# Weight tiles kept in HBM as float32r parts, and an ordering model with other matmul durations and one resource shared by DVE's SBUF and POOL's operations

## The chip, the cores and the metric

The kernel runs on one core of a Trainium2 chip. The metric is the time of one execution on the device in microseconds, the median of several runs.

## The reference

Four sequences of 576 positions pass through three layers in a row.

- Attention: 8 heads of 64 features; scores `q k^T / 8`, a causal mask, and a bias `min(-(cum_i - cum_j), 0)` from the running sum of `max(s, 0)`; a softmax; the product with `v`.
- A layer norm over 512 features with a gain, `max(xn @ w1a, 0) @ w2a` with 2048 hidden features, added to x (below: layer 0).
- A mixer along the sequence, `u = x + (x^T U V)^T` with rank 32, then `max(u @ w1b, 0) @ w2b`, added to u (below: layer 1).

The weights and U and V arrive as float64, the rest as float32. The result is float32.

```python
x = np.ascontiguousarray(attn_out.transpose(0, 2, 1, 3)).reshape(B, S, H * D)
x = _moe_ref(x=x, **moe_kwargs)       # layer norm, then x + relu(xn @ w1) @ w2
return _moe2_ref(x=x, **moe2_kwargs)  # u = x + (x^T U V)^T, then u + relu(u @ w1) @ w2
```

## The kernel before

The work is cut into eight blocks: each sequence has a part A of 256 positions and a part B of 320. A step is one block with one of the 16 weight tiles of a layer (128 hidden features): `mlp1` makes the hidden features, `mlp2`, two steps behind it (`LAG`), adds them into the output. `GROUPS` lists the order: layer 0 of A0, A1, A2, B0 and A3, layer 1 of A0 and B0 together, layer 0 of B1 and B2, layer 1 of A1 and B1, layer 0 of B3, and layer 1 of the rest, 256 steps in all. Each run takes first the half of the weights that is on chip from the run before, and so loads eight tiles per 16 steps (or per 32, where two blocks run together).

Products are made in float32r, a shorter float that TensorE takes at full pace. To keep the accuracy, a number is split in a high part and a low part (the rest), and a product takes three matmuls: high by high, low by high, high by low (lines 1013 to 1015 in `mlp1`, 1047 to 1049 in `mlp2`). A step has 24 of them. The first two steps take plain float32 (`FULL_STEPS`).

A weight tile has two halves (of w1 and of w2), each 128 x 512. Eight tiles (`WSLOTS`, 16 buffers `w` of a high and a low part) are on chip. A half comes on chip in one of two ways:

- *Fresh*: the raw float64 is loaded (`w_raw`, 512 KB, lines 479 and 481, buffers `wr`), turned to float32 by five operations (`f64_to_f32`, lines 459 to 469: one on ACT or DVE, two on DVE (462, 466), one on ACT (464), and an integer addition on POOL (469)) in a buffer `wt`, and split: the high part is a rounding copy on ACT (343) or DVE (344), the low part a subtraction on POOL (350) or DVE (348). If the tile is used again, the float32 in `wt` is also stored to an HBM buffer `w_dr` (256 KB, line 521).
- *Reloaded*: the float32 is loaded from `w_dr` into a `wt` (256 KB, line 502) and split again.

The first eight tiles of layer 1 (`early`) are converted ahead of time, beside layer 0 (`w_convert`, from step 44 on; layer 1 begins at step 80), and stored (line 491), and their first use is a reload.

Beside the steps runs the rest: attention of the next blocks (scores into PSUM, bias, mask on POOL, maximum on DVE in line 658, exponential on ACT, transposes, the product with v), the layer norms and the mixer. `AT` and `LN` say beside which steps.

Nothing of this is issued in program order. `Plan` records each operation with the engines that may take it and a duration on each (`alts`), and what it reads and writes. `Plan.plan` then runs a model: at each turn the earliest operation that can start is issued, by priority among the ready ones. Where several engines may take one, the one that ends first is chosen, with a price per engine and 10 us window added. `issue` plans once, and then up to six times (`PASSES`) more with the latest starts of the last plan as priorities and with prices moved so that DVE, ACT and POOL are used evenly in each window; the shortest plan is issued. Each engine then works its operations off in that order and waits on semaphores. All DMAs are issued by one queue, SP's, in the order of the plan; in the model a DMA takes 1.1 us and its bytes at 360 per ns. A load has a `gate`: it is not issued ahead of a certain step.

The model knows a matmul as

```python
def mm_cost(n):
    return max(106.7, n / 2.4) + 2.5
```

and treats DVE and POOL as independent of each other. A buffer becomes free when all recorded users of the old tile in it are done; the next tile's first operation waits for that. For `wt` the user is the split, for `w` the last matmul that reads the tile.

Of the kernel before, what the change touches and what calls it, by code (L numbers as in the profile page):

```python
# [9 lines left out]
F32 = mybir.dt.float32  # L10
# [32 lines left out]
def mm_cost(n):  # L43
    return max(106.7, n / 2.4) + 2.5
# [15 lines left out]
WIN, NW = 10e3, 110  # L60


class Buf:
    """A tile that is allocated when the first operation on it is issued."""
# [14 lines left out]
class Op:  # L79
    __slots__ = ("prio", "alts", "deps", "after", "wait", "ready", "bufs", "start", "end", "soft", "eng", "slots", "nbytes", "seq", "gate")  # L80


class Plan:
    """Records operations in program order, then issues them in the order in which a model of
    the engines finds them ready, by priority where several are."""
# [53 lines left out]
    def plan(self, prio, price):  # L139
        """The order in which a model of the engines finds the operations ready, by priority where several are."""  # L140
# [36 lines left out]
        while avail:  # L177
# [3 lines left out]
            for o in avail:  # L181
                fin = None
                for e, (dur, _) in o.alts.items():
                    s = slot(o, e)
                    if s is None:
                        continue
                    s = max(s, o.ready[e])
                    f0 = max(s, tent.get(e, 0.0)) + dur
                    if len(o.alts) > 1:
                        f0 += price[e][min(int(s / WIN), NW - 1)] * dur + (o.soft if e == "dve" else 0.0)  # L190
                    if fin is None or f0 < fin[0]:
                        fin = (f0, max(s, free[e]), e, dur)
# [3 lines left out]
                if fin[1] <= tent.get(e, 0.0):  # L196
                    tent[e] = tent.get(e, 0.0) + fin[3]
# [40 lines left out]
    def latest(self, order, end):  # L238
        """Latest starts that keep the end and the tensor engine's order."""
# [16 lines left out]
    def issue(self, warm):  # L256
        """Plans several times, with the latest starts of the last plan as priorities and engines' prices
        that even their use out, and issues the shortest plan."""
        self.link()
        price = {e: [0.0] * NW for e in ("act", "pool", "pe", "sp")}  # L260
        price["dve"] = [1.0] * NW
        shared = ("dve", "act", "pool")
# [3 lines left out]
        for _ in range(PASSES):  # L266
            prio = self.latest(order, end)
            use = {e: [0.0] * NW for e in price}
            for o, e, *_ in order:
                use[e][min(int(o.start / WIN), NW - 1)] += o.alts[e][0] / WIN  # L270
# [12 lines left out]
        for o, e, s, t, new in best:  # L283
            # Before the first MLP, the tensor engine's gaps are filled, so that its clock stays up.
# [14 lines left out]
def mha_ffn_mixer_ffn(ctx: ExitStack, tc, qkv_p, qkv_a, qkv_b, s, g, w1, w2, U, V, out):  # L299
# [26 lines left out]
    def dve(prio, n, fn, reads, writes, rate=1.042, fixed=68):  # L326
        P.op(prio, {"dve": (fixed + rate * n, fn)}, reads, writes)
# [13 lines left out]
    def copy(prio, n, out, a, reads, writes, psum=False, soft=0.0, slow=False):  # L341
# [3 lines left out]
        }, reads, writes, soft=soft)  # L345

    def tt(prio, n, out, a, b, op, reads, writes, psum=False, soft=0.0):
# [3 lines left out]
        P.op(prio, alts, reads, writes, soft=soft)  # L351
# [85 lines left out]
    for n, it in enumerate(inst):  # L437
        k = (it["l"], it["m"])
        it["fresh"], it["keep"] = k not in seen, False
        if k in seen:  # L440
            inst[seen[k]]["keep"] = True
            if k not in w_dr:
                w_dr[k] = P.fixed(dr_p.tile([128, 1024], F32, name=f"w_dr{k[0]}_{k[1]}"))
# [4 lines left out]
    early = [(1, m) for m in range(HALF)]  # L448
    for it in inst:
        if (it["l"], it["m"]) in early:  # L450
            it["fresh"] = False

    def f64_to_f32(prio, n, dst, raw, bd, br, words=(0, 1)):
        """Bits of float64 in word pairs, rounded to float32."""
# [6 lines left out]
        }, [(br, words[1])], [bd])  # L461
# [24 lines left out]
    def w_convert(prio, l, m, half, gate):  # L486
        raw = w_raw(prio, l, m, half, gate)
        src = P.buf("wt", [128, 512])
        f64_to_f32(prio, 512, lambda: src.tile, lambda: raw.tile, src, raw)
        sl = slice(512 * half, 512 * (half + 1))  # L490
        load(prio, 128 * 2048, lambda: nc.sync.dma_start(w_dr[l, m][:, sl], src.tile), [src], [(w_dr[l, m], half)])

    def w_load(n, half, gate):
# [3 lines left out]
        sl = slice(512 * half, 512 * (half + 1))  # L497
        if it["fresh"]:
            raw = w_raw(prio, l, m, half, gate)
        else:  # L500
            raw = P.buf("wt", [128, 512])
            load(prio, 128 * 2048, lambda: nc.sync.dma_start(raw.tile, w_dr[l, m][:, sl]), [(w_dr[l, m], half)], [raw], gate)
        it["raw", half] = raw

    def w_split(n, half):
        it = inst[n]
        l, m = it["l"], it["m"]
        prio = it["first"] - 4
        src = it.pop(("raw", half))
        sl = slice(512 * half, 512 * (half + 1))  # L510
        if it["fresh"]:
            if it["full"]:
                w = it["w", half] = it["w", 0] if half else P.buf("w", [128, 2, 512])
# [677 lines left out]
```

## Time and profile before

| | before |
|---|---|
| median of 3 runs | 1199.7 us (1198.89 to 1199.91) |
| profiled execution, first to last instruction | 1201.9 us |
| TensorE (PE) busy | 1119.7 us, 7801 matmuls |
| VectorE (DVE) busy | 874.7 us |
| ScalarE (ACT) busy | 652.4 us |
| GpSimd (POOL) busy | 605.7 us |
| DMA | 177.44 MB, mean 148 GB/s |
| mean granted TensorE clock | 0.974 |

The page gives no other time of the profiled execution than its span, so the span stands for it; it is 2.2 us over the median. Busy time of an engine counts from an instruction's start to its end, waits for a resource inside an instruction included. A matmul's end is modelled, and matmuls overlap. The words in front of and behind `<-` are the buffer written and the buffers read: `w<-wt,w` is a split, `wt<-wr` a conversion, `wt<-w_dr` a reload.

### The profile page before, as it was taken

Reading aid. Unit: us, or ns where it says so; the run is one execution under the profiler, and the core shown is the slowest. Engines: PE = TensorE matmul, PEld = TensorE weight load, DVE = VectorE, ACT = ScalarE, POOL = GpSimd, SP = SyncE. Lnnn points to the kernel's source line nnn. Section 1 sums busy time; section 2 is a strip of 40 time slices with the busy share of each in tenths; the row PEclk is TensorE's granted clock in tenths of the full one; section 3 lists DMA queues with packets and bytes.
Section 4 is the critical chain, followed back from the end, with each engine's and each line's share of the span. In section 5 each row is a group of like instructions: output and inputs, shape, how many; then the busy total and the mean of one; then the engine's idle time right before and its main releaser. Section 6 shows DMA issues by size and latency. Waiting matters only on the chain.

```text
span 1201.9 us, 22316 instructions
## 1 busy us (share of the span) xinstructions
PE 1119.7 (93%) x7801; PEld 1049.2 (87%) x7801; DVE 874.7 (73%) x1947; ACT 652.4 (54%) x1484; POOL 605.7 (50%) x717
## 2 busy tenths in 40 slices
PE   8798787998889998998899999999999999999998
PEld 5567687887888988897789898989999999999998
DVE  6999999998997998979997857696664443313232
ACT  5657576786666766756577646474533342312221
POOL 4666666775566665736755644354441362201300
PEclk8879899999999999999899999999999999999999
DMA  6466657334475746526634431734214453311111
GB/s 215 161 229 215 215 193 224 100 132 160 139 241 167 249 166 220 177 78 220 218 102 167 150 109 65 247 120 159 71 54 140 163 173 100 114 45 63 64 43 40
DMA packets 80639, 177.44 MB, mean 148 GB/s; under 512 B 10064, under 2 KB 17744, under 8 KB 80528
## 3 DMA queue, kind: packets, MB, share of 16 engines
q1 hardware_dynamic: 80528, 176.03, 43.7%
q8 instruction: 61, 1.00, 0.3%
q14 instruction: 50, 0.41, 0.1%
HBM read 147.61 MB, written 28.39 MB: 146 GB/s over the span
## 4 chain that ended last, share of the span: by engine, by line
PE 53%; DVE 30%; issue 6%; ACT 5%; DMA 4%; POOL 2%; SPq 0%; POOLq 0%; DVEq 0%; ACTq 0%
PE ps L1013 8%; PE ps L1014 7%; PE ps L1015 7%; PE acc L1047 5%; PE acc L1049 5%; PE acc L1048 5%; DVE t L658 4%; PE ps L1047 2%; PE ps L1048 2%; PE ps L1049 2%; DVE wt L466 2%; PE ps L750 2%; DVE t L612 2%; DVE w L348 2%; DVE hl L1020 2%
## 5 line engine op out<-in xcount | busy, mean ns | idle before, releaser
L350 POOL TENSOR_TENSOR w<-wt,w 128x512 fp32r<-128x512 f32 x173 | 234.8, 1363 | 205.7 <-ACT w L343 122.0
L1013 PE MATMUL ps<-xh,w 128*128 128x256 f32 (+1 forms) x1016 | 314.8, 310 | 2.6 <-DVE mx L658 1.2
L1015 PE MATMUL ps<-xl,w 128*128 128x256 f32 (+1 forms) x1016 | 303.4, 299 | 1.2 <-DVE xl L348 0.9
L1014 PE MATMUL ps<-xh,w 128*128 128x256 f32 (+1 forms) x1016 | 303.1, 298 | 0.0
L1020 DVE SCALAR_TENSOR_TENSOR hl<-ps,hh 128x256 fp32r<-128x256 f32 (+1 forms) x254 | 115.5, 455 | 206.8 <-ACT hh L1019 204.9
L1019 ACT ACTIVATE hh<-ps 128x256 fp32r<-128x256 f32 (+1 forms) x254 | 103.2, 406 | 281.8 <-PE ps L1015 280.3
L1047 PE MATMUL acc<-hh,w 128*128 128x256 f32 (+1 forms) x760 | 230.0, 303 | 6.8 <-DVE x L1057 4.2
L1049 PE MATMUL acc<-hl,w 128*128 128x256 f32 (+1 forms) x760 | 224.6, 296 | 9.1 <-DVE hl L1020 9.0
L1048 PE MATMUL acc<-hh,w 128*128 128x256 f32 (+1 forms) x760 | 223.4, 294 | 0.0
L1013 PEld LDWEIGHTS ps<-xh,w 128*128 128x128 f32 x1016 | 195.0, 192 | 9.4 <-issue 2.4
L1015 PEld LDWEIGHTS ps<-xl,w 128*128 128x128 f32 x1016 | 195.0, 192 | 2.0 <-DVE xl L348 1.3
L1014 PEld LDWEIGHTS ps<-xh,w 128*128 128x128 f32 x1016 | 195.1, 192 | 0.9 <-issue 0.2
L1049 PEld LDWEIGHTS acc<-hl,w 128*128 128x128 f32 x760 | 146.4, 193 | 11.2 <-DVE hl L1020 11.2
L1047 PEld LDWEIGHTS acc<-hh,w 128*128 128x128 f32 x760 | 146.3, 193 | 9.8 <-ACT hh L1019 6.8
L343 ACT ACTIVATE w<-wt 128x512 fp32r<-128x512 f32 x208 | 125.9, 625 | 41.6 <-POOL wt L469 24.7
L1048 PEld LDWEIGHTS acc<-hh,w 128*128 128x128 f32 x760 | 146.5, 193 | 0.5
L670 ACT ACTIVATE t<-t,mx 64x576 f32<-64x576 f32 (+3 forms) x160 | 95.9, 600 | 64.1 <-POOL mx L666 35.2
L469 POOL TENSOR_TENSOR wt<-wt,wr 128x512 int32<-128x512 int32 (+2 forms) x71 | 98.7, 1391 | 50.0 <-DVE wt L466 14.4
L348 DVE TENSOR_TENSOR w<-wt,w 128x512 fp32r<-128x512 f32 x111 | 99.8, 908 | 5.7 <-ACT w L343 4.0
L653 PE MATMUL ps<-kv,q 128*128 128x288 f32 (+4 forms) x320 | 71.2, 337 | 13.4 <-DVE q L348 4.2
L1047 PE MATMUL ps<-hh,w 128*128 128x320 f32 x256 | 79.3, 310 | 0.0
L1049 PE MATMUL ps<-hl,w 128*128 128x320 f32 x256 | 79.3, 310 | 0.0
(149 smaller groups left out, 2133.8 us busy)
## 6 DMA issues: line engine op xcount, KB each, us to landing
wt<-w_dr SPq DMA_DIRECT2D x232, 256.0 KB, 3.0
raw<-qkv_b SPq DMA_DIRECT2D x32, 608.0 KB, 4.6
w_dr<-wt SPq DMA_DIRECT2D x64, 256.0 KB, 2.6
wr<-w1a SPq DMA_DIRECT2D x20, 512.0 KB, 4.2
wr<-w2a SPq DMA_DIRECT2D x20, 512.0 KB, 4.1
nckb<-nck_dr SPq DMA_DIRECT2D x32, 288.0 KB, 5.3
wr<-w1b SPq DMA_DIRECT2D x16, 512.0 KB, 4.8
wr<-w2b SPq DMA_DIRECT2D x16, 512.0 KB, 5.0
```

Source lines behind the costliest of these rows:

```text
L343: "act": ((51 if psum else 94) + 0.8333 * n, lambda: nc.scalar.activation(out(), a(), AF.Copy)),
L348: alts = {"dve": (68 + 1.042 * n, lambda: nc.vector.tensor_tensor(out=out(), in0=a(), in1=b(), op=op))}
L350: alts["pool"] = (148 + 2.104 * n, lambda: nc.gpsimd.tensor_tensor(out=out(), in0=a(), in1=b(), op=op))
L469: P.op(prio, {"pool": (148 + 2.104 * n, lambda: nc.gpsimd.tensor_tensor(out=dst().bitcast(I32), in0=dst().bitcast(I32), in1=pair(0).bitcas ...
L1013: nc.tensor.matmul(ps[:, :n], w[:, 0, sl], xh[:, k, :n], start=k == 0, stop=False)
L1014: nc.tensor.matmul(ps[:, :n], w[:, 1, sl], xh[:, k, :n], start=False, stop=False)
L1015: nc.tensor.matmul(ps[:, :n], w[:, 0, sl], xl[:, k, :n], start=False, stop=k == KT - 1)
L1019: act(st - 1000, n, lambda: nc.scalar.activation(hh[:, :n], ps[:, :n], AF.Relu), [ps], [hh], 51)
L1020: dve(st - 1000, n, lambda: nc.vector.scalar_tensor_tensor(out=hl[:, :n], in0=ps[:, :n], scalar=0.0, in1=f(hh[:, :n]), op0=ALU.max, op1=AL ...
L1047: nc.tensor.matmul(a, w[:, 0, sl], hh[:, :n], start=new, stop=False)
L1048: nc.tensor.matmul(a, w[:, 1, sl], hh[:, :n], start=False, stop=False)
L1049: nc.tensor.matmul(a, w[:, 0, sl], hl[:, :n], start=False, stop=last and (z == 1 or blk == "B"))
```

## The change

- `w_load` of a tile that is not fresh now allocates the buffer `w` and loads both parts into it in one DMA of 512 KB; nothing is computed. `w_dr` has room for the two parts of the two halves.
- `w_split` of a fresh tile converts and splits as before and then stores both parts from `w` (512 KB) if the tile is used again. The store of the plain float32 is gone, also for the tiles of the first two steps.
- `w_convert`, `early` and the steps that ran it are gone: the first use of each tile of layer 1 is fresh.
- `mm_cost` adds 13.3 instead of 2.5.
- An operation has a set `port`: the engines on which it holds a shared resource called "port". POOL holds it in every operation, DVE in those that read no PSUM buffer (marked by the helpers, or by hand where an operation is recorded directly). In the model, two operations that hold it never run at the same time. The prices even out DVE, ACT and the port instead of DVE, ACT and POOL; DVE's price starts at 0.5 instead of 1; and there are 130 windows instead of 110.
- Comments and texts of documentation were taken out.

The model decides the order in which instructions are issued on each engine, and on which engine some of them run. The core of the diff:

```diff
 def mm_cost(n):
-    return max(106.7, n / 2.4) + 2.5
+    return max(106.7, n / 2.4) + 13.3
...
-WIN, NW = 10e3, 110
+WIN, NW = 10e3, 130
...
-    def op(self, prio, alts, reads=(), writes=(), nbytes=0, gate=None, soft=0.0, hold=()):
+    def op(self, prio, alts, reads=(), writes=(), nbytes=0, gate=None, soft=0.0, hold=(), port=False):
         o = Op()
+        o.port = {e for e in alts if e == "pool" or (e == "dve" and port)}
...
-                    f0 = max(s, tent.get(e, 0.0)) + dur
+                    port = e in o.port
+                    f0 = max(s, tent.get(e, 0.0), tent.get("port", 0.0) if port else 0.0) + dur
                     if len(o.alts) > 1:
-                        f0 += price[e][min(int(s / WIN), NW - 1)] * dur + (o.soft if e == "dve" else 0.0)
+                        w = min(int(s / WIN), NW - 1)
+                        f0 += (price[e][w] + (price["port"][w] if port else 0.0)) * dur + (o.soft if e == "dve" else 0.0)
                     if fin is None or f0 < fin[0]:
-                        fin = (f0, max(s, free[e]), e, dur)
+                        fin = (f0, max(s, free[e], free["port"] if port else 0.0), e, dur)
...
             free[e] = o.end
+            if e in o.port:
+                free["port"] = o.end
...
-        price = {e: [0.0] * NW for e in ("act", "pool", "pe", "sp")}
-        price["dve"] = [1.0] * NW
-        shared = ("dve", "act", "pool")
+        price = {e: [0.0] * NW for e in ("act", "pool", "pe", "sp", "port")}
+        price["dve"] = [0.5] * NW
+        shared = ("dve", "act", "port")
...
     def dve(prio, n, fn, reads, writes, rate=1.042, fixed=68):
-        P.op(prio, {"dve": (fixed + rate * n, fn)}, reads, writes)
+        on_chip = not any((b[0] if isinstance(b, tuple) else b).tag in ("ps", "acc") for b in reads)
+        P.op(prio, {"dve": (fixed + rate * n, fn)}, reads, writes, port=on_chip)
...
-    early = [(1, m) for m in range(HALF)]
-    for it in inst:
-        if (it["l"], it["m"]) in early:
-            it["fresh"] = False
...
     def w_load(n, half, gate):
         it = inst[n]
         l, m = it["l"], it["m"]
-        prio = it["first"] - 4
-        sl = slice(512 * half, 512 * (half + 1))
         if it["fresh"]:
-            raw = w_raw(prio, l, m, half, gate)
-        else:
-            raw = P.buf("wt", [128, 512])
-            load(prio, 128 * 2048, lambda: nc.sync.dma_start(raw.tile, w_dr[l, m][:, sl]), [(w_dr[l, m], half)], [raw], gate)
-        it["raw", half] = raw
+            it["raw", half] = w_raw(it["first"] - 4, l, m, half, gate)
 
-    def w_split(n, half):
+    def w_split(n, half, gate):
...
+        dr = w_dr.get((l, m))
+        if not it["fresh"]:
+            w = it["w", half] = P.buf("w", [128, 2, 512], F32R)
+            load(prio, 128 * 4096, lambda: nc.sync.dma_start(f(w.tile), dr[:, half]), [(dr, half)], [w], gate)
+            return
+        raw = it.pop(("raw", half))
+        if it["full"]:
+            w = it["w", half] = it["w", 0] if half else P.buf("w", [128, 2, 512])
+            f64_to_f32(prio, 512, lambda: w[:, half], lambda: raw.tile, (w, half), raw)
+            return
+        w = it["w", half] = P.buf("w", [128, 2, 512], F32R)
+        t = P.buf("wt", [128, 512])
+        f64_to_f32(prio, 512, lambda: t.tile, lambda: raw.tile, t, raw)
+        split(prio, 512, lambda: w[:, 0], lambda: w[:, 1], lambda: t.tile, [t], [(w, 0)], [(w, 1)])
+        if it["keep"]:
+            load(prio, 128 * 4096, lambda: nc.sync.dma_start(dr[:, half], f(w.tile)), [w], [(dr, half)])
...
-    for n, (l, m) in enumerate(early):
-        for half in range(2):
-            put(start1 - 36 + 3 * (n + half / 2), lambda p, g, l=l, m=m, half=half: w_convert(p, l, m, half, g))
```

## Rows read from the trace of the kernel before

**Rows 1.** The page: busy shares, and the chain that ended last.

```profile
PE 1119.7 (93%) x7801; PEld 1049.2 (87%) x7801; DVE 874.7 (73%) x1947; ACT 652.4 (54%) x1484; POOL 605.7 (50%) x717
...
PE 53%; DVE 30%; issue 6%; ACT 5%; DMA 4%; POOL 2%; SPq 0%; POOLq 0%; DVEq 0%; ACTq 0%
```

**Rows 2.** Stretch, length, busy us (count) PE PEld DVE ACT POOL, PEclk, DMA, GB/s.

```profile
0.00:180.00 180.00, 150.37 (x917) 121.31 (x918) 164.92 (x379) 114.47 (x300) 115.53 (x129) 0.89 0.62 205
180.00:420.00 240.00, 215.83 (x1534) 199.86 (x1533) 216.98 (x525) 166.57 (x396) 160.24 (x201) 0.99 0.53 176
420.00:600.00 180.00, 162.62 (x1153) 152.82 (x1152) 162.85 (x328) 112.97 (x238) 112.58 (x132) 0.96 0.54 181
600.00:900.00 300.00, 292.37 (x2028) 277.74 (x2027) 224.73 (x521) 177.81 (x377) 147.22 (x200) 1.00 0.37 125
900.00:1200.00 300.00, 298.46 (x2179) 297.49 (x2177) 105.23 (x200) 80.63 (x175) 70.13 (x57) 1.00 0.28 94
540.00:600.00 60.00, 49.17 (x326) 46.73 (x325) 58.30 (x99) 35.50 (x73) 41.30 (x37) 0.91 0.65 219
840.00:900.00 60.00, 60.00 (x446) 58.79 (x445) 38.29 (x91) 29.14 (x64) 24.69 (x28) 1.00 0.19 65
```

**Rows 3.** Timeline, 555 to 563: start, length, engine, line, operation [idle before].

```profile
555.42 0.68 DVE L466 SCALAR_TENSOR_TENSOR wt<-wr,wt 128x512 uint32<-128x512 uint32 x1
...
556.23 1.38 POOL L469 TENSOR_TENSOR wt<-wt,wr 128x512 int32<-128x512 int32 x1 [2.20 <-ACT xc L843]
...
556.76 1.40 DVE L466 SCALAR_TENSOR_TENSOR wt<-wr,wt 128x512 uint32<-128x512 uint32 x1
...
558.12 0.28 PE L1013 MATMUL ps<-xh,w 128*128 128x256 f32 x1
...
558.24 0.28 PE L1014 MATMUL ps<-xh,w 128*128 128x256 f32 x1
...
558.84 0.31 PE L1047 MATMUL acc<-hh,w 128*128 128x320 f32 x1
...
558.99 0.31 PE L1048 MATMUL acc<-hh,w 128*128 128x320 f32 x1
```

**Rows 4.** Groups by form: line, engine, names, shapes, count | busy, mean ns | idle.

```profile
L350 POOL TENSOR_TENSOR w<-wt,w 128x512 fp32r<-128x512 f32 x173 | 234.8, 1363 | 205.7 <-ACT w L343 122.0 <-DVE w L344 45.5 <-DVE hl L1020 25.1
...
L343 ACT ACTIVATE w<-wt 128x512 fp32r<-128x512 f32 x208 | 125.9, 625 | 41.6 <-POOL wt L469 24.7 <-DMA wt<-w_dr 15.7 <-PE ps L1049 0.4
...
L348 DVE TENSOR_TENSOR w<-wt,w 128x512 fp32r<-128x512 f32 x111 | 99.8, 908 | 5.7 <-ACT w L343 4.0
...
L469 POOL TENSOR_TENSOR wt<-wt,wr 128x512 int32<-128x512 int32 x68 | 96.5, 1420 | 47.8 <-DVE wt L466 13.5 <-ACT wr L464 4.8 <-issue 4.8
...
L466 DVE SCALAR_TENSOR_TENSOR wt<-wr,wt 128x512 uint32<-128x512 uint32 x68 | 60.6, 893 | 0.6
...
L344 DVE CAST w<-wt 128x512 fp32r<-128x512 f32 x76 | 44.5, 589 | 8.6 <-PE ps L1015 4.6 <-DMA wt<-w_dr 2.5 <-POOL wt L469 1.2
...
L462 DVE TENSOR_SCALAR wt<-wt 128x512 uint32<-128x512 uint32 x68 | 44.3, 654 | 5.0 <-ACT wt L459 4.8
```

**Rows 5.** Line 502 in 180 to 420, then 600 to 900: issues, times.

```profile
L502 SPq DMA_DIRECT2D wt<-w_dr x44: 319/320/433, 190.9 to 419.7; - x44
...
L502 SPq DMA_DIRECT2D wt<-w_dr x80: 319/320/889, 605.2 to 882.1; - x80
```

**Rows 6.** Waits of the SP queue: total us, times, longest.

```profile
SPq L502 <- POOL w L350: 225.3, 88, 21.0
SPq L1061 <- DVE x L1057: 136.4, 17, 24.5
```

**Rows 7.** DMA issues: count, KB each, median us to landing.

```profile
wt<-w_dr SPq DMA_DIRECT2D x232, 256.0 KB, 3.0
...
w_dr<-wt SPq DMA_DIRECT2D x64, 256.0 KB, 2.6
...
wr<-w2b SPq DMA_DIRECT2D x16, 512.0 KB, 5.0
```

More of the change, by code (lines that the diff above doesn't have):

```diff
@@ L79 @@
 class Op:
-    __slots__ = ("prio", "alts", "deps", "after", "wait", "ready", "bufs", "start", "end", "soft", "eng", "slots", "nbytes", "seq", "gate")
+    __slots__ = ("port", "prio", "alts", "deps", "after", "wait", "ready", "bufs", "start", "end", "soft", "eng", "slots", "nbytes", "seq", "gate")
 class Plan:
@@ L195, in plan @@
                 e = fin[2]
-                if fin[1] <= tent.get(e, 0.0):
-                    tent[e] = tent.get(e, 0.0) + fin[3]
+                for g in (e, "port") if e in o.port else (e,):
+                    if fin[1] <= tent.get(g, 0.0):
+                        tent[g] = tent.get(g, 0.0) + fin[3]
                 if e not in best:
@@ L269, in issue @@
             for o, e, *_ in order:
-                use[e][min(int(o.start / WIN), NW - 1)] += o.alts[e][0] / WIN
+                w = min(int(o.start / WIN), NW - 1)
+                use[e][w] += o.alts[e][0] / WIN
+                if e in o.port:
+                    use["port"][w] += o.alts[e][0] / WIN
             for w in range(NW):
@@ L344, in copy @@
             "dve": (68 + (1.042 if psum or slow else 0.521) * n, lambda: nc.vector.tensor_copy(out(), a())),
-        }, reads, writes, soft=soft)
+        }, reads, writes, soft=soft, port=not psum)
     def tt(prio, n, out, a, b, op, reads, writes, psum=False, soft=0.0):
@@ L350, in tt @@
             alts["pool"] = (148 + 2.104 * n, lambda: nc.gpsimd.tensor_tensor(out=out(), in0=a(), in1=b(), op=op))
-        P.op(prio, alts, reads, writes, soft=soft)
+        P.op(prio, alts, reads, writes, soft=soft, port=not psum)
     def split(prio, n, hi, lo, src, reads, wh, wl, psum=False, soft=0.0, slow=False):
@@ L442, in mha_ffn_mixer_ffn @@
             if k not in w_dr:
-                w_dr[k] = P.fixed(dr_p.tile([128, 1024], F32, name=f"w_dr{k[0]}_{k[1]}"))
+                w_dr[k] = P.fixed(dr_p.tile([128, 2, 2, 512], F32, name=f"w_dr{k[0]}_{k[1]}"))
         elif n >= 4:
@@ L508, in w_split @@
         prio = it["first"] - 4
[L509 to L513, printed above, removed]
-                f64_to_f32(prio, 512, lambda: w[:, half], lambda: src.tile, (w, half), src)
-                if it["keep"]:
-                    load(prio, 128 * 2048, lambda: nc.sync.dma_start(w_dr[l, m][:, sl], w[:, half]), [(w, half)], [(w_dr[l, m], half)])
-                return
-            raw, src = src, P.buf("wt", [128, 512])
-            f64_to_f32(prio, 512, lambda: src.tile, lambda: raw.tile, src, raw)
-            if it["keep"]:
-                load(prio, 128 * 2048, lambda: nc.sync.dma_start(w_dr[l, m][:, sl], src.tile), [src], [(w_dr[l, m], half)])
-        w = P.buf("w", [128, 2, 512], F32R)
-        split(prio, 512, lambda: w[:, 0], lambda: w[:, 1], lambda: src.tile, [src], [(w, 0)], [(w, 1)])
-        it["w", half] = w
+        dr = w_dr.get((l, m))
[14 more added lines that the diff above has]
+            load(prio, 128 * 4096, lambda: nc.sync.dma_start(dr[:, half], f(w.tile)), [w], [(dr, half)])
     xt = {}
@@ L845, in layer_norm @@
                                                                             scalar2=None, op0=ALU.mult)),
-            }, [(xc, k), g_sb], [(xc, k)])
+            }, [(xc, k), g_sb], [(xc, k)], port=True)
         y, z = P.buf("ls", [128, 320]), P.buf("ls", [128, 320])
@@ L1087, in w_step @@
     def w_step(k, gate):
-        w_split(*halves[k])
+        w_split(*halves[k], gate)
         w_next(k + 2, gate)
```

16 lines of the change are left out of this document (5 added, 11 removed).

## The prediction

> **What bounds the kernel now.** I read the busy shares and the chain of waits first. TensorE (PE) is busy 93% of the span, and the chain that ended last lies 53% on PE and 30% on VectorE (DVE) [rows 1]. So PE sets the end, but DVE makes it late for a good part of the time. Next I read the table by stretch, to see where. From 900 us on PE is busy 298.5 of 300 us and nothing else matters; before 600 us DVE is at 90% or more of each stretch [rows 2].
>
> Busy time flatters PE, because a matmul's record covers its latency. The timeline shows the real pace: starts 0.12 us apart for 256 columns and 0.15 for 320 [rows 3] (0.120 and 0.147 in the unrounded starts). I took the usual interval of each form, over all 7801 matmul starts, and summed what lies above it. That is PE's loss: 63 us in 0 to 180, 47 in 180 to 420, 35 in 420 to 600, 25 in 600 to 900, and 1 after 900, 171 in all. The matmul counts agree: 446 matmuls fit into 840 to 900, where PE is busy throughout, 0.134 us each, and the 1534 of 180 to 420 would need 206 of their 240 us [rows 2]. Spells at the lower granted clock (0.89 on average before 180, 0.91 in 540 to 600) are inside the loss.
>
> The loss follows DVE's load [rows 2]. Per 60 us it is 2.3 us where DVE is at 64% (840 to 900), 5.0 at 75% (600 to 900), 11.7 at 90% (180 to 600), and 18 at 97% (540 to 600). I use these four points as the price list.
>
> Part of DVE's load is waiting. At 556.76 an L466 starts while POOL is in an L469 that ends at 557.61; it ends at 558.16 and takes 1.40 us, where the same instruction took 0.68 just before [rows 3]. So DVE, working on SBUF alone, stood until POOL was done. Over the trace L466 averages 0.893 and the split's subtraction on DVE 0.908 [rows 4], against 0.68 and 0.69 when free. Over L344, L348, L462 and L466 the excess makes about 68 us.
>
> **What is removed.** 232 half tiles are reloaded as float32 and split again (a rounding to the high part, a subtraction for the low part). 16 of them become first uses that are converted and split on the spot, and 216 come back as finished parts. There are 284 splits now: the high part 208 times on ACT at 0.625 and 76 times on DVE at 0.589, the low part 173 times on POOL at 1.363 and 111 times on DVE at 0.908 [rows 4]. 216 of 284 is 76%, so ACT loses 99 us, DVE 111 and POOL 179. Per reload that is 0.51 us of DVE and 0.83 of POOL. What it is worth depends on the stretch.
>
> **180 to 420 us (loss 47).** 44 reloads lie here [rows 5]: 22 us of DVE go. The early conversion of layer 1's first eight tiles also goes from here, 16 halves with 0.654 + 0.893 of DVE each [rows 4], 25 us. POOL becomes emptier by 59 us of 160, for which I give DVE 6 us of waits back. DVE falls from 217 to 164 us, which is 79% of a stretch of some 210 us, and the price list says 6.5 us per 60, or 22. Gain 25. Bounds: 10, if PE's stalls here are the dependences of attention and not DVE's queue; 37, if the loss falls to the rate of 840 to 900.
>
> **600 to 900 us (loss 25).** 80 reloads [rows 5], 41 us of DVE, and 8 of waits: 225 becomes 176, 62%, a loss of 10. Gain 15, bounds 5 and 22.
>
> **420 to 600 us (loss 35).** Here work is added. Layer 1's first eight tiles are no longer ready in HBM; they are loaded raw, converted and split in the few steps ahead of their use, as the second eight already are in 540 to 600. That is 25 us of DVE and 16 times 1.42 us of POOL [rows 4]. About 15 other reloads give 8 us back. DVE would stand at 180 of 188 us, 96%, and the price list gives 53 us, 18 worse. From the other side: the L466 of rows 3 shows that half of such an operation can be waiting, and an order that counts the shared resource can take that out, so no loss at all is possible, even a gain of 10. I take 9 worse, the middle, because neither end has a row of its own.
>
> **0 to 180 us (loss 63).** No reload lies here (the first is at 190.9 [rows 5]), so only the ordering model acts. It now prices a matmul at 120 ns for 256 columns (106.7 + 13.3), which is the pace of rows 3, where it had 109. And it keeps an SBUF operation of DVE and any operation of POOL apart, which is what rows 3 show. A plan that fits the machine better puts PE's side work where its inputs are ready, and it makes the low part dear on POOL (1.3 us of the shared resource against 0.69 on DVE). But it is a greedy search, and another input may give a worse order. I take 8 gained, with bounds of 10 lost and 25 gained.
>
> **Transfers.** 216 loads and 64 stores go from 256 to 512 KB: 280 x 0.262 = 73 MB; the 16 reloads that fall away take 4 back. 177 MB become 246. In 540 to 600, 219 GB/s made a share of 0.65 [rows 2], so a full share is some 337 GB/s (estimate), and the mean becomes 213. This hides under PE except where three refills follow each other without pause, at 900 to 985: a refill is 16 halves, 8.4 MB, in eight B steps of 24 x 0.147 = 3.5 us, so 300 GB/s, just under the limit. I take 1 us, with bounds of 0 and 12.
>
> **The new wait.** A reload used to go into a wt buffer and waited there for its split; now it goes straight into the w slot, so the SP queue stands until PE's last matmul on the old tile. Behind it in that one queue are the q/k/v and bias loads of attention, and the stores. SP waits now too: 225 us in 88 waits for POOL's subtraction, and once 24.5 us for an output [rows 6]. A slot falls free two steps after its last use and is wanted eight steps after that use, so some five steps remain, 5 x 24 x 0.12 = 14 us. A 512 KB raw tile lands 5.0 us after its issue [rows 7]. I price this at nothing, with 9 us of room as the cover.
>
> **Sum.** 8 + 25 - 9 + 15 - 1 = 38. The profiled execution took 1201.9, so 1163.9; the median lies 2.2 lower, at 1199.7, which makes 1162.
>
> A rule of the Trainium skill bears on the waits: SBUF — State Buffer, section Who interferes with whom, says that DVE and GpSimd share a port pair as an exclusive lock for a whole instruction, and that the loser blocks fully. Rows 3 agree (the wait ended with POOL's instruction, not by slowing both). Taken at its word, the waits shrink with POOL's share, by 179 of 606, so 20 of the 68 us go where I gave 14, and with an order that avoids them entirely all 68 would; the sum would be some 4 to 15 us lower, 1147 to 1158.
>
> **The rivals.**
> - *The order is the main thing.* If the planner, with true prices, also empties the start and carries the conversions, the stretches give 25 + 35 + 10 + 18 = 88, so 1112. For it: all losses lie where DVE and POOL queue on each other. Against it: in 0 to 180 DVE is at 165 of 180 us, with its conversions unchanged [rows 2].
> - *The load was not the cause.* PE waits for chains of short hops; then less load brings only the lower bounds, 10 + 5 - 8 = 7, so 1193. For it: even at 64% DVE some loss is left. Against: it grows fivefold from there to 90%.
> - *Nothing changes* (1200): the reload of 900 to 1200 was hidden anyway, and the conversions eat the rest.
> - *Late reloads, slower.* The SP queue stands at a slot, the attention loads behind it come late, PE falls back, and the slot comes later still. 216 halves are 13.5 refills; at 5 us each, one landing time, this costs 68, so 1162 + 68 = 1230. It turns the gain into a loss from 2.8 us a refill on. For it: SP's waits of up to 24.5 us [rows 6]. Against: the 9 us of room.
>
> **How the numbers follow.** The forecast has 0.57 (1140 to 1185 by its own bounds), the main-order rival 0.16, the little-gain rival 0.14, no change 0.05, late reloads 0.08. Faster is 0.57 + 0.16 + 0.14 = 0.87. About 0.2% is what can be told from no change here (the three runs spread over 0.09%). The range goes from 1112 to 1196: outside are half of the first rival (0.08), no change (0.05) and late reloads (0.08).
>
> **What would show it.** L350 and L343 on w some 70 times each at most, and DVE below 80% in the stretch of blocks A2 to A3. Mean L466 and L348 near 0.7 us if the order keeps the two engines apart. A loss of 40 to 45 us around the first group of layer 1. PE without gaps in the last 300 us. Wrong would be: PE waits released by loads into w, or SP waits for PE that grow beyond 10 us; or a start (before the first reload) that moved by more than 25 us either way.

## The result and the profile after

The changed kernel takes 1159.05 us (median of 4 runs, 1155.53 to 1160.90) where the kernel before took 1199.47 on the same chip: ratio 0.9653, interval 0.9629 to 0.9676. Its profiled execution took 1159.34 us with a span of 1157.5, 44.4 less than the span of before. By the medians the gain is 40.4: in every run with both on record the time is about 1.8 us above the span, so the execution profiled before, with its span of 1201.9, took some 1203.7 us (estimate), 4 above its median.

The page after (busy shares, DMA, chain), against [rows 1]:

```profile
PE 1103.0 (95%) x7808; PEld 1045.3 (90%) x7808; DVE 703.3 (61%) x1733; ACT 608.4 (53%) x1422; POOL 314.7 (27%) x561
...
DMA packets 78332, 246.63 MB, mean 213 GB/s; under 512 B 9808, under 2 KB 17488, under 8 KB 78224
...
PE 72%; DVE 10%; ACT 7%; DMA 5%; issue 3%; POOL 2%; SPq 0%; POOLq 0%; ACTq 0%; DVEq 0%
```

DVE lost 171 us of busy time, POOL 291, and DVE's part of the chain fell from 30% to 10%, PE's rose from 53% to 72%. The bytes are the 246 MB of the prediction.

The windows after, against [rows 2] (same columns; the same times hold later steps now):

```profile
0.00:180.00 180.00, 154.59 (x994) 128.32 (x995) 147.59 (x388) 140.68 (x364) 85.78 (x113) 0.93 0.76 259
180.00:420.00 240.00, 235.36 (x1767) 225.78 (x1766) 174.71 (x470) 158.43 (x393) 85.63 (x190) 1.00 0.63 219
420.00:600.00 180.00, 161.06 (x1094) 150.16 (x1093) 159.55 (x354) 139.31 (x288) 89.04 (x129) 0.95 0.76 266
600.00:900.00 300.00, 298.33 (x2092) 288.34 (x2091) 158.52 (x389) 130.09 (x284) 48.32 (x124) 1.00 0.58 202
900.00:1140.00 240.00, 240.00 (x1778) 239.30 (x1778) 59.65 (x128) 38.59 (x92) 5.90 (x7) 1.00 0.46 159
```

DVE is at 73% in 180 to 420, where it was at 90%, and PE starts 1767 matmuls there in place of 1534. In 420 to 600 the sides are turned: fewer matmuls than before (1094 to 1153), and a granted clock of 0.95.

The groups of the conversion and the split after, against [rows 4] (L466 is L472 now, L462 is L468, L469 is L475, L343, L344, L348 and L350 are L353, L354, L358 and L360):

```profile
L475 POOL TENSOR_TENSOR wt<-wt,wr 128x512 int32<-128x512 int32 x68 | 97.3, 1433 | 101.1 <-DVE wt L472 50.9 <-issue 12.8 <-ACT t L604 4.8
...
L472 DVE SCALAR_TENSOR_TENSOR wt<-wr,wt 128x512 uint32<-128x512 uint32 x68 | 52.4, 773 | 0.2
...
L358 DVE TENSOR_TENSOR w<-wt,w 128x512 fp32r<-128x512 f32 x60 | 49.8, 833 | 2.1 <-ACT w L353 1.7
...
L468 DVE TENSOR_SCALAR wt<-wt 128x512 uint32<-128x512 uint32 x68 | 39.5, 589 | 5.7 <-ACT wt L465 5.4
...
L353 ACT ACTIVATE w<-wt 128x512 fp32r<-128x512 f32 x56 | 34.7, 623 | 13.0 <-POOL wt L475 12.7
...
L360 POOL TENSOR_TENSOR w<-wt,w 128x512 fp32r<-128x512 f32 x8 | 10.3, 1293 | 3.1 <-ACT w L353 3.1
...
L354 DVE CAST w<-wt 128x512 fp32r<-128x512 f32 x12 | 5.6, 468 | 1.5 <-POOL wt L475 1.5
```

68 splits are left of 284, and 60 of their 68 subtractions lie on DVE; before it was 111 of 284. The same conversion got shorter: L472 0.773 where it was 0.893, L468 0.589 where it was 0.654, and the subtraction L358 0.833 where it was 0.908. So DVE waits less for POOL within its instructions, but the means are not near the 0.7 that the prediction named as a sign. Counted as in the prediction (over L344, L348, L462, L466 and what stands in their place, mean less 0.42, 0.69, 0.42 and 0.68), it is 27 us over 208 instructions, 0.13 each; before it was 68 over 323, 0.21 each.

Where the time went is best read by steps, since the same step stands at another time in each run. The next table has, from the starts of the matmuls of `mlp1`, how long each part of the program took in the profiled execution (us): steps 0 to 24 (no reload in them), 24 to 72 (the prediction's 180 to 420), 72 to 104 (420 to 600), 104 to 168 (600 to 900), and the rest.

```
                    0-24   24-72  72-104  104-168   rest    span
before             183.9   255.2   152.4    308.1  302.3  1201.9
after              173.7   227.2   156.7    296.5  303.4  1157.5
difference         -10.2   -28.0    +4.3    -11.6   +1.1   -44.4
predicted             -8     -25      +9      -15     +1     -38
parts_alone        184.1   231.2   166.4    299.7  302.3  1183.7
model_alone        165.6   233.7   148.7    294.1  302.3  1144.4
after_mm25         169.8   224.5   152.2    294.6  303.1  1144.2
after_noport       192.2   236.0   161.2    304.7  303.7  1197.8
parts_early        173.0   226.0   140.2    294.4  303.0  1136.6
model_alone_mm25   171.9   239.0   143.3    296.9  302.3  1153.4
dve_load           172.0   259.8   157.4    313.1  303.4  1205.7
copy_more          170.3   235.0   162.5    306.3  317.3  1191.4
price_1            171.7   230.8   150.8    295.2  303.1  1151.6
parts_early_mm25   171.1   226.1   154.7    292.1  303.1  1147.1
parts_early_p12    172.3   225.8   140.7    294.3  303.0  1136.1
load_half_more     172.3   313.2   186.7    450.8  478.5  1601.6
```

PE's loss, measured as in the prediction, is 130 us after (58, 19, 39, 14 and 1 by stretch) where it was 171. The five terms of the sum have the right signs and lie within 5 us of the table, in which the differences from before add up to 4 us more than the medians give. What they come from is another matter, and the experiments were made for that.

### The profile page after: what moved, and what is told of

The parts are those of the page before. It is cut to its first block, busy times and chain, and to the rows that moved or that the text cites. A ratio compares the mean times of both kernels' runs of the same rounds, so it can differ in the third digit from the quotient of the medians.

```text
span 1157.5 us, 21778 instructions
## 1 busy us (share of the span) xinstructions
PE 1103.0 (95%) x7808; PEld 1045.3 (90%) x7808; DVE 703.3 (61%) x1733; ACT 608.4 (53%) x1422; POOL 314.7 (27%) x561
## 4 chain that ended last, share of the span: by engine, by line
PE 72%; DVE 10%; ACT 7%; DMA 5%; issue 3%; POOL 2%; SPq 0%; POOLq 0%; ACTq 0%; DVEq 0%
PE ps L1007 10%; PE ps L1008 10%; PE ps L1009 10%; PE acc L1041 7%; PE acc L1042 7%; PE acc L1043 7%; PE ps L744 3%; PE ps L647 3%; PE ps L1043 3%; PE ps L1042 3%; PE ps L1041 3%; PE ps L700 2%; ACT t L664 2%; DMA nckb<-nck_dr 1%; DMA wr<-w1a 1%
## 5 line engine op out<-in xcount | busy, mean ns | idle before, releaser
L475 POOL TENSOR_TENSOR wt<-wt,wr 128x512 int32<-128x512 int32 (+2 forms) x71 | 99.5, 1403 | 102.3 <-DVE wt L472 50.9
L617 POOL TENSOR_SCALAR_AFFINE_SELECT t<-t 128x128 f32<-128x128 f32 (+1 forms) x128 | 49.5, 388 | 133.2 <-ACT t L604 86.5
L652 DVE CUSTOM_DVE_ANT_0 t<-ps,t 64x288 f32<-64x288 f32 (+3 forms) x160 | 73.3, 479 | 12.3 <-PE ps L647 8.7
L1042 PE MATMUL ps<-hh,w 128*128 128x320 f32 x256 | 79.1, 309 | 0.0
L1041 PE MATMUL ps<-hh,w 128*128 128x320 f32 x256 | 79.0, 309 | 0.0
L647 PE MATMUL ps<-kv,q 128*128 128x288 f32 (+4 forms) x320 | 68.6, 332 | 8.0 <-DVE kv L358 4.0
```

What stands on the lines that cost most here:

```text
L475: P.op(prio, {"pool": (148 + 2.104 * n, lambda: nc.gpsimd.tensor_tensor(out=dst().bitcast(I32), in0=dst().bitcast(I32), in1=pair(0).bitcas ...
L647: nc.tensor.matmul(ps[:, p0:p0 + k1 - k0], q[:, z, c0:c0 + 128], kv[:, k0:k1], start=z == 0, stop=z == 1)
L652: nc.vector.tensor_tensor_reduce(out=t[r0:r1, o + k0:o + k1], in0=ps[r0:r1, p0:p0 + k1 - k0], in1=t[r0:r1, o + k0:o + k1], scale=0.125, sc ...
L1041: nc.tensor.matmul(a, w[:, 0, sl], hh[:, :n], start=new, stop=False)
L1042: nc.tensor.matmul(a, w[:, 1, sl], hh[:, :n], start=False, stop=False)
```

## Experiments

Two theories: the load of the splits on DVE and POOL made PE late (the prediction's main part), or the order in which DVE and POOL meet each other did (its first rival). The first four runs take the change apart.

**The finished parts alone.** The changed kernel with the old model:

```diff
-    return max(106.7, n / 2.4) + 13.3
+    return max(106.7, n / 2.4) + 2.5
...
-WIN, NW = 10e3, 130
+WIN, NW = 10e3, 110
...
-        o.port = {e for e in alts if e == "pool" or (e == "dve" and port)}
+        o.port = set()
...
-        price["dve"] = [0.5] * NW
-        shared = ("dve", "act", "port")
+        price["dve"] = [1.0] * NW
+        shared = ("dve", "act", "pool")
```

> The finished parts in HBM alone; the ordering model is that of before (2.5 ns, no shared resource, DVE's price from 1, 110 windows). If the load of the splits made the loss: the terms of the stretches without the start, 25 + 15 - 9 - 1 = 30 us, so some 1169 (1160 to 1180). If the order is the main thing: little of it, 1185 to 1200, with the subtraction on DVE still above 0.85 us.

Measured 1187.50 us, ratio 0.9894 (0.9872 to 0.9917): only 11 us. The groups show DVE's waits as they were before (L472 0.926, L358 0.955; in all four groups 41 us over 191 instructions, 0.21 each):

```profile
L472 DVE SCALAR_TENSOR_TENSOR wt<-wr,wt 128x512 uint32<-128x512 uint32 x68 | 62.7, 926 | 0.8
...
L358 DVE TENSOR_TENSOR w<-wt,w 128x512 fp32r<-128x512 f32 x32 | 30.4, 955 | 0.9 <-ACT w L353 0.6
```

By steps, 24 to 72 gain 24 where 25 were predicted, 104 to 168 gain 8 where it was 15, and the start and the rest nothing. But steps 72 to 104, with the late conversion, lose 14 and eat half or more. (These add up to 18 and not to 11, since the execution profiled before was a long one and the one profiled here took 1185.51, 2 under its median.) Neither theory gave this time: it is between the two.

**The model alone.** The changed kernel with the weights of before: float32 in `w_dr`, reloads into `wt` that are split again, and `early` with `w_convert`.

```diff
+    early = [(1, m) for m in range(HALF)]
+    for it in inst:
+        if (it["l"], it["m"]) in early:
+            it["fresh"] = False
...
+        w = P.buf("w", [128, 2, 512], F32R)
+        split(prio, 512, lambda: w[:, 0], lambda: w[:, 1], lambda: src.tile, [src], [(w, 0)], [(w, 1)])
```

> The new ordering model alone; the weights are stored as float32, reloaded and split again, and layer 1's first eight tiles converted ahead, as before. If the load made the loss: only the start's 8 us and some of the waits, 1185 to 1195. If the order is the main thing: 1160 to 1175.

Measured 1145.32 us, ratio 0.9546 (0.9527 to 0.9565), below both expectations. With all 284 splits still in it, it gains 54 us, more than the whole change, which the load theory cannot give. The groups show how:

```profile
L358 DVE TENSOR_TENSOR w<-wt,w 128x512 fp32r<-128x512 f32 x207 | 156.3, 772 | 12.4 <-ACT w L353 10.0
...
L360 POOL TENSOR_TENSOR w<-wt,w 128x512 fp32r<-128x512 f32 x77 | 102.5, 1334 | 175.7 <-ACT w L353 102.5 <-PE acc L1057 53.2 <-DVE w L354 14.7
...
L476 DVE SCALAR_TENSOR_TENSOR wt<-wr,wt 128x512 uint32<-128x512 uint32 x68 | 53.9, 794 | 0.5
```

The planner took 207 of the subtractions to DVE, where one holds the shared resource some 0.7 us and not 1.33, and L358 takes 0.772 on average; over the four groups DVE waits 0.10 us per instruction, 37 us over 382. So the model changed not the order alone but also the choice of engine, and POOL's busy time fell from 605.7 us to 403.5. That POOL is emptier does not explain the shorter waits: in parts_alone and in after_noport (the changed kernel without the resource, below) POOL is about as empty, and DVE waits 0.21 and 0.24 us per instruction. From the pages of model_alone, parts_alone and after_noport:

```profile
PE 1098.4 (96%) x7854; PEld 1038.9 (91%) x7854; DVE 815.0 (71%) x1892; ACT 716.0 (63%) x1623; POOL 403.5 (35%) x633
```

```profile
PE 1108.3 (94%) x7820; PEld 1048.3 (89%) x7820; DVE 755.2 (64%) x1750; ACT 578.0 (49%) x1343; POOL 421.6 (36%) x623
```

```profile
PE 1119.2 (93%) x7820; PEld 1058.3 (88%) x7820; DVE 775.4 (65%) x1798; ACT 563.4 (47%) x1312; POOL 387.5 (32%) x606
```

No run keeps the choice of engine and changes only the order, so the two are not told apart in the time. The windows of model_alone:

```profile
180.00:420.00 240.00, 229.20 (x1663) 215.05 (x1663) 211.20 (x528) 185.57 (x432) 133.24 (x210) 0.99 0.56 183
600.00:900.00 300.00, 298.83 (x2101) 290.32 (x2100) 205.21 (x463) 175.08 (x365) 66.83 (x133) 1.00 0.40 134
```

In 180 to 420 DVE is nearly as full as before (211 of 240 us, 217 in [rows 2]), and PE makes 1663 matmuls in place of 1534.

**The matmul duration** and **the shared resource**, each taken out of the changed kernel:

```diff
-    return max(106.7, n / 2.4) + 13.3
+    return max(106.7, n / 2.4) + 2.5
```

> The changed kernel with the old matmul duration (2.5 ns added instead of 13.3). If a matmul of 109 ns makes PE's side work come too early: PE waits more in the start and around 420 to 600, 1168 to 1180. If only the shared resource matters in the model: 1155 to 1164.

Measured 1147.02 us, ratio 0.9556 (0.9526 to 0.9586): 12 us better without the duration that fits. Neither expectation held.

```diff
-        o.port = {e for e in alts if e == "pool" or (e == "dve" and port)}
+        o.port = set()
...
-        shared = ("dve", "act", "port")
+        shared = ("dve", "act", "pool")
```

> The changed kernel with the shared resource taken out of the model (prices even out DVE, ACT and POOL again), the new matmul duration kept. If keeping the two engines apart is what removed DVE's waits: the conversion's L472 goes back to 0.85 to 0.9 us on average and the time to 1170 to 1185. If the waits went because the splits went: 1155 to 1164 and L472 near 0.75.

Measured 1199.32 us, ratio 0.9999 (0.9982 to 1.0016): nothing is left of the gain, parts and all. That is more than the first expectation had; its sign of the waits, L472 at 0.85 to 0.9, came.

```profile
L472 DVE SCALAR_TENSOR_TENSOR wt<-wr,wt 128x512 uint32<-128x512 uint32 x68 | 64.0, 941 | 0.8
...
L468 DVE TENSOR_SCALAR wt<-wt 128x512 uint32<-128x512 uint32 x68 | 45.8, 675 | 0.8 <-ACT wt L465 0.2
```

Both are back at the level of before or above it (0.893 and 0.654 in [rows 4]); over the four groups 48 us over 200 instructions, 0.24 each. So the shared resource in the model carries the change. All plans say the same: those made with the resource, here and below, take 1137.70 to 1159.05 us (where no transfers or load are added), and the three made without it 1187.50, 1199.32 and 1199.47. No other setting of the planner that was varied moves the time by more than 12. The waits in these groups are not the whole of it: price_1 below takes 1154.51 with 0.17 per instruction, the changed kernel 1159.05 with 0.13.

A part of the gains comes by TensorE's clock. Matmuls of 256 columns start 0.120 us apart at the higher of its two levels (2.4 GHz) and 0.213 at the lower (1.2 GHz), and a fall can follow waits of PE: in the changed kernel PE is busy 14.7 of the 20 us from 440 on, and the granted clock is 0.76 in the 20 after that. By the traces 212 matmuls start at the lower level before, 159 after, 56 in model_alone and 278 in after_noport. At 0.093 us each that is some 20, 15, 5 and 26 us (estimate).

The next four ask what the parts cost on top of the new model (1145.32 without them, 1159.05 with them).

**The early conversion put back**, with both parts stored:

```diff
+    early = [(1, m) for m in range(HALF)]
+    for it in inst:
+        if (it["l"], it["m"]) in early:
+            it["fresh"] = False
...
+    def w_convert(prio, l, m, half, gate):
+        raw = w_raw(prio, l, m, half, gate)
+        t, hi = P.buf("wt", [128, 512]), P.buf("wt", [128, 512], F32R)
+        f64_to_f32(prio, 512, lambda: t.tile, lambda: raw.tile, t, raw)
+        split(prio, 512, lambda: hi.tile, lambda: t.tile.bitcast(F32R), lambda: t.tile, [t], [hi], [t])
+        for z, x in enumerate((hi, t)):
+            load(prio, 128 * 2048, lambda z=z, x=x: nc.sync.dma_start(w_dr[l, m][:, half, z], f(x.tile)), [x], [(w_dr[l, m], half)])
...
+    for n, (l, m) in enumerate(early):
+        for half in range(2):
+            put(start1 - 36 + 3 * (n + half / 2), lambda p, g, l=l, m=m, half=half: w_convert(p, l, m, half, g))
```

> The changed kernel with the early conversion put back: layer 1's first eight tiles are converted and split from step 44 on, both parts stored (256 KB each), and the first use is a reload. If the late conversion is what the parts cost on top of the model: steps 72 to 104 take 148 us again instead of 157, in all 1146 to 1152. If the difference is only another outcome of the greedy search: no such change in steps 72 to 104, anywhere from 1143 to 1165.

Measured 1137.70 us, ratio 0.9476 (0.9451 to 0.9501): the fastest of all, below what was expected and 8 us below the model alone. Steps 72 to 104 take 140 us in place of 157, and the other parts move by 2 at most, so between these two plans it is the late conversion. PE's waits for splits of weights in these steps are 6.9 us in the changed kernel and 0.6 here. The old matmul duration tells otherwise, though: there (after_mm25 and, below, parts_early_mm25) these steps take 152 with the late conversion and 155 with the early one, with 10.4 and 3.1 us of such waits. So the waits come with the late conversion, and what they cost in time depends on the plan. In the changed kernel's timeline (start, length, engine, line) one sees PE stand for it:

```profile
438.21 0.90 DVE L472 SCALAR_TENSOR_TENSOR wt<-wr,wt 128x512 uint32<-128x512 uint32 x1
...
439.19 1.41 POOL L475 TENSOR_TENSOR wt<-wt,wr 128x512 int32<-128x512 int32 x1 [0.63 <-DVE wt L472]
...
439.37 1.78 DVE L358 TENSOR_TENSOR w<-wt,w 128x512 fp32r<-128x512 f32 x1
...
441.20 0.39 PE L1008 MATMUL ps<-xh,w 128*128 128x256 f32 x1 [0.29 <-DVE w L358]
```

The subtraction of a fresh split (439.37, 1.78 us) waits for POOL's conversion of the next half (439.19 to 440.60), and PE waits for the subtraction (the matmul at 441.20). The window 420 to 480, first of the changed kernel and then of this one:

```profile
420.00:480.00 60.00, 49.29 (x319) 43.77 (x318) 53.37 (x105) 49.63 (x100) 34.83 (x44) 0.90 0.84 295
```

```profile
420.00:480.00 60.00, 59.70 (x459) 57.17 (x458) 47.75 (x116) 41.57 (x88) 18.96 (x44) 1.00 0.65 251
```

319 matmuls there, 459 here, at full clock.

**More transfers.** One more DMA for each reload, in the same order:

```diff
+            def go():
+                nc.sync.dma_start(f(w[:, 0]), dr[:, half, 0])
+                nc.sync.dma_start(f(w.tile), dr[:, half])
```

> The changed kernel in the same order, with one more DMA of 256 KB (the high part, into its own place) before each of the 216 reloads: 57 MB more, where the change itself added 69. If transfers hide under PE, as the prediction priced them: 1157 to 1163. If they cost: the added 57 MB cost about what the change's 69 MB did, 1168 to 1180, with PE released by DMAs into w.

Measured 1602.96 us, ratio 1.3349 (1.3306 to 1.3391). This is not a test of bytes: both write the same buffer, so the SP queue stood until the first had landed, 3.65 us in each of 216 reloads.

```profile
SPq L508 <- DMA w<-w_dr: 789.4, 216, 6.6
```

```profile
PE ps L1011 <- DMA w<-w_dr: 133.7, 35, 7.2
```

But it does what the prediction's slower rival supposed: reloads that hold up their queue made PE wait for tiles, and the run longer by 444 us, 33 per refill, at a mean granted clock of 0.865 (896 matmuls start at its lower level). The mechanism exists; the change did not trigger it.

And one more DMA that nothing waits for:

```diff
+            def go():
+                nc.sync.dma_start(f(w.tile), dr[:, half])
+                spare = dr_p.tile([128, 512], F32, name=f"spare{n}_{half}")
+                nc.sync.dma_start(spare, dr.tile[:, half, 0])
```

> The changed kernel in the same order, with a DMA of 256 KB behind each of the 216 reloads that copies a high part from HBM to a spare place in HBM, of its own each time: 57 MB read and written beside the rest, and nothing reads it. If transfers hide under PE, as the prediction priced them: 1157 to 1163. If they cost by their bytes (the change itself added 69 MB): 1166 to 1180.

Measured 1195.70 us, ratio 0.9973 (0.9949 to 0.9997): 37 us for 57 MB, above both expectations. A reload lands after 7.9 us where it took 6.1:

```profile
w<-w_dr SPq DMA_DIRECT2D x216, 512.0 KB, 7.9
...
spare<-w_dr SPq DMA_DIRECT2D x216, 256.0 KB, 7.9
```

```profile
SPq L507 <- DMA w<-w_dr: 93.4, 117, 2.2
...
SPq L509 <- DMA spare<-w_dr: 45.0, 115, 2.1
```

14 of the 34 us by steps lie in the rest, where three refills follow each other and PE had stood nowhere. So more transfers of this kind are not free. What they used up is open. It can be the bytes: from 900 to 1000 us, where the three refills lie, 350 GB/s are moved in place of 256. It can be the number of DMAs: the DMAs of this program use eight semaphores in turn, so each waits until the eighth before it has landed (the waits in the last fence, 138 us), and 335 of 753 were issued within 0.3 us of that landing, where it was 28 of 537 in the changed kernel. Nor does a copy within HBM have to cost what a load into SBUF costs; no run adds bytes to the loads alone.

**More load in the same order:**

```diff
+    scr = fixed("scr", [128, 256])
...
+            def go():
+                nc.sync.dma_start(f(w.tile), dr[:, half])
+                for _ in range(2):
+                    nc.vector.tensor_tensor(out=scr.tile, in0=scr.tile, in1=scr.tile, op=ALU.max)
```

> The changed kernel in the same order, with two more DVE operations on an SBUF tile of their own (128x256, some 0.42 us each) at each of the 216 reload issues: 181 us more of DVE and of the shared resource, where the parts took 111 of DVE and 179 of POOL away. If loss follows DVE's load (the price list): DVE from 61% to 77%, 20 to 30 us over 180 to 900, so 1179 to 1189. If what counts is when the two engines meet and not how much they do: under 1168.

Measured 1209.89 us, ratio 1.0075 (1.0049 to 1.0100): 51 us over the changed kernel, more than expected.

```profile
180.00:420.00 240.00, 219.36 (x1557) 205.26 (x1555) 197.13 (x523) 145.43 (x361) 81.41 (x177) 0.98 0.52 176
600.00:900.00 300.00, 287.44 (x1966) 269.51 (x1965) 236.09 (x600) 147.50 (x320) 64.18 (x155) 1.00 0.55 193
```

DVE is at 82% and 79% here, and PE loses 44 and 33 us in these stretches, where the price list of the prediction has 33 and 34. POOL does the same as in the changed kernel, and over the four groups DVE waits 0.12 us per instruction, no more than there. So load that the order does not know of is paid at that list, or over it (it stands in the middle of a fixed order, so its amount and its place are not told apart). Load that it knows of is cheaper: the model alone has DVE at 88% in 180 to 420 and PE loses 32, where the list has 43; in parts_early, with DVE at 85% there, PE loses 23, where it has 38.

**How much is the outcome of the search?** Three runs change one setting of the planner, a fourth gives it more passes.

```diff
-    return max(106.7, n / 2.4) + 13.3
+    return max(106.7, n / 2.4) + 2.5
```

in the model alone:

> The new model alone without its matmul duration: the weights as before, 2.5 ns added, the shared resource kept. If the matmul duration worsens the order in itself (with the parts it cost 12 us): 1133 to 1140. If that was chance, or bound to the parts: 1142 to 1150. If the duration is what helped here: above 1155.

Measured 1152.88 us, ratio 0.9602 (0.9575 to 0.9629): 8 us worse, between the ranges expected. And with the parts and the early conversion:

> Parts, early conversion and the shared resource, with the old matmul duration. If 2.5 ns suits the parts (12 us were gained by it without the early conversion): 1126 to 1132. If that gain was chance, or the same time as the late conversion cost: 1134 to 1150.

Measured 1148.15 us, ratio 0.9564 (0.9543 to 0.9586): 10 us worse. In the changed kernel itself the old duration was 12 us better. DVE's price from 1.0, in the changed kernel:

```diff
-        price["dve"] = [0.5] * NW
+        price["dve"] = [1.0] * NW
```

> The changed kernel with DVE's price started at 1.0 as before, nothing else: a probe of what another outcome of the search is worth. If a model that fits is what counts and the search adds little: 1155 to 1163. If outcomes of the search differ by what the matmul duration did (12 us one way, 8 the other): anywhere from 1143 to 1172.

Measured 1154.51 us, ratio 0.9625 (0.9609 to 0.9641): up to 5 us better, which the intervals of the two ratios (0.9629 to 0.9676 for the changed kernel) hardly separate. And twelve passes in place of six, with the parts and the early conversion:

```diff
-PASSES = 6
+PASSES = 12
```

> Parts with the early conversion and both parts of the new model, and twelve more passes of the planner instead of six, of which the shortest plan is issued. If the model tells plans apart: not above 1138. If plans within some 10 us are the same to it: 1130 to 1148.

Measured 1139.14 us, ratio 0.9496 (0.9474 to 0.9518). In the traces the instructions of PE, DVE, ACT and POOL stand in the same order as in parts_early, so the same plan was issued: six more passes found none that the model holds for shorter. It is a second measurement of one plan, 1.4 us from the first, and tells nothing of how well the model tells plans apart. The matmul duration moves the time by 8 to 12 us, better in one program and worse in the two others. So a single outcome of the search is worth some 10 us either way, and no run shows the duration to help or to harm by itself.

## Why the prediction was right, and where its reasons were not

The time (1162 against 1159), the sign and the five terms came out, the terms to within 5 us of the table. What made the time is not what the prediction said, and that the sum fits is luck.

- **The start** (8 gained): 10. The model alone gave 18, within the bound of 25.
- **180 to 420** (25 gained): 28. The load worked out from the counts agrees with the parts by themselves: 24 (19 in after_noport). But the model by itself gives 22 here with the splits in it, and both together 28. The two do not add. A reason that fits, though no run shows it for the time, is that both take away the same waits: of DVE's 68 us in the four groups the parts take 27, the model 31, and both together 41.
- **600 to 900** (15 gained): 12. Alone, the parts give 8 and the model 14, so these do not add either.
- **420 to 600** (9 lost): 4. It is a difference of two larger things. Steps 72 to 104 lose 14 with the parts under the old model, and the late conversion 16.5 under the new one (157 against 140), which is near the price list's 18 and nearly twice what I took; but with the old matmul duration it costs nothing (152 against 155). The model gains 4 here by itself.
- **Transfers** (1 lost): 1. The same prices, though, would have hidden the copies, which cost 37.
- **The new wait** (nothing): the sign that I named, SP waiting for PE longer than 10 us, is there:

```profile
SPq L506 <- PE ps L1009: 121.7, 64, 19.1
...
SPq L506 <- PE ps L1043: 95.4, 61, 5.2
```

It was a bad sign. A queue that waits 19.1 us for a slot does no harm as long as the tile arrives in time, and PE waits for a load into w only once, 1.3 us. For splits of weights it waits some 13 of the 51 us that it stands idle; the two longest of these in total, and the load:

```profile
PE acc L1042 <- DVE w L358: 4.6, 5, 1.8
...
PE ps L1008 <- DVE w L358: 4.2, 6, 1.7
...
PE ps L1007 <- DMA w<-w_dr: 1.3, 1, 1.3
```

A 512 KB tile lands after 6.1 us, not 5.0 as in [rows 7], which leaves 8 of the 14 us of room and not 9:

```profile
w<-w_dr SPq DMA_DIRECT2D x216, 512.0 KB, 6.1
...
w_dr<-w SPq DMA_DIRECT2D x64, 512.0 KB, 5.0
...
wr<-w2b SPq DMA_DIRECT2D x16, 512.0 KB, 6.4
```

The step that failed is the use of the price list. I read loss against DVE's load in a kernel whose order did not know the shared resource, and took the load for the cause. Without the resource in the model the parts gain 11 us (1187.50) or nothing (1199.32); with it and without the parts the gain is 54 (1145.32). But 30 of the 38 us were written down to the weights (25 - 9 + 15 - 1) and 8 to the model, and the rival that the order is the main thing, to which I gave 0.16, names the cause; its time (1112) was wrong, because it kept the weights' gains beside the order's. The number came out because 54 gained by the model, with 14 lost where these parts are put on top of it, is about what 8 and 30 add up to. What the parts are worth on top of the model is not settled: with the new matmul duration they lose 14, or gain 8 with the early conversion; with the old duration they gain 5 or 6 either way; none of these is clearly more than the outcome of a search is worth.

The Trainium skill's rule, in SBUF — State Buffer, section Who interferes with whom, is that whichever of the two engines issues first holds the shared pair for its whole instruction. The runs agree that it matters when the two meet: the waits went from 0.21 us per instruction to 0.10 in the model alone, with all splits still there. The sum that the prediction gave by that rule, 1147 to 1158, ended just below the 1159.05, but it rests on the same 30 us for the parts, so no run shows it to be better founded.

Some steps of the prediction are loose without changing the result. The 2.2 us between its span and its median belong to the one execution that was profiled. 164 of 210 us is 78% and not 79%. The first rival's 35 and 18 are not the bounds of the stretches (37 and 22), and the 8 that the second rival takes off has no working.

The range's lower part would have been needed for parts_early (1137.70), which beats both kernels: 0.9476 of the time before, against 0.9653.

## What to carry to other kernels

When an engine is full, ask first how much of its busy time is waiting inside its instructions: the same instruction's shortest and mean durations tell. Where two engines hold a resource in turn, an order that knows it can be worth more than taking work away, and the two gains do not add. And work moved from idle steps to the steps just ahead of its use can cost more than it saves, even where the total falls: here it cost 16.5 us in one plan and nothing in another, so try it early too. Last, before one plan of a greedy search is compared with another, find out what a mere change of settings does to the time: here some 10 us.

## What the runs showed of the hardware

- A DVE operation on SBUF that met one of POOL did not slow down, it stood until the other had ended: 0.68 us alone and 1.40 us when started in the middle of POOL's [rows 3], 1.78 us in the timeline after. The same subtraction with one input in PSUM did not wait: 32 of them averaged 0.684 us in the kernel before, where those on SBUF alone averaged 0.908 [rows 4]. No run tells which of the operations on SBUF have to wait; the model takes all of them.

```profile
L348 DVE TENSOR_TENSOR pB<-ps,pB 128x512 fp32r<-128x512 f32 x32 | 21.9, 684 | 2.6 <-ACT pB L343 2.6
```

- 57 MB more, read and written by 216 copies within HBM, beside a mean of 213 GB/s without them, made a 512 KB load land after 7.9 us in place of 6.1, and cost 37 us. Whether by bytes or by the number of DMAs in flight stays open.
